# Attention and two expert layers on one core: the attention's last outputs and routing a tile sooner, fewer warm transposes, and split products in another order

## The chip, the cores and the metric

The kernel runs on one core of a Trainium2 chip. The metric is the device time of one execution in microseconds, as the median of several runs. The engines are named as in the profile: PE (TensorE), DVE (VectorE), ACT (ScalarE), POOL (GpSimd) and SP (the queue that issues most DMAs).

## The reference

Three layers stand behind one another. The attention is clustered: 2 batches, 8 heads, 768 tokens of 64 features, and a query sees only the keys whose nearest of 16 centroids is its own. Then every token goes to one of 8 experts (capacity 384), and a gated layer follows.

```python
q_assign = np.argmax(np.einsum('bhsd,hcd->bhsc', q_n, c_n), axis=-1)
k_assign = np.argmax(np.einsum('bhsd,hcd->bhsc', k_n, c_n), axis=-1)
mask = q_assign[:, :, :, None] == k_assign[:, :, None, :]
scores = np.where(mask, scale * np.matmul(q, k.transpose(0, 1, 3, 2)), -1000000000.0)
attn = softmax(scores)
x = np.matmul(attn, v)                       # (1536 tokens, 512)
logits = x @ w_gate                          # 8 experts
expert_idx = np.argmax(logits, axis=1)
...
h = np.maximum(np.einsum('ecd,edf->ecf', disp, w1), 0.0)
y = np.einsum('ecf,efd->ecd', h, w2)         # out[i] = gate_w[i] * y[...]
...
g = x @ w_gate; val = x @ w_val              # gated layer, 1536 wide
out = (g * sigmoid(g) * val) @ w_out
```

## The kernel before, in words

The order of the work is written out by hand; each engine runs its instructions in the order in which the program issues them.

**Start** (`Attention.run`, from line 430). After 16 warm transposes on PE (`warm`, line 424, transposes of the identity whose result nobody reads), `tr0` (line 166) transposes q and then k of the first pair of heads and makes three copies of each: X, in full precision, for the cluster assignment; H, the rounded high part; and L = X - H, on POOL. `moves` copies H and L into the operands Aq, qB, Ak and kB by DMA on SP's queue. `assign0` multiplies X with the centroids and makes a one-hot on DVE, `tr0` does the second pair's q, 28 more warm transposes follow, and `mask0` (line 259) transposes the one-hot (tile otp) and writes it into qB and kB as extra rows that mask the scores. Then the loop starts.

**The loop** (from line 491) goes over 96 tiles g of 128 queries; a group of three tiles is half a head, and eight pairs of heads make 96. In each tile the tokens of `CFG["order"]` are worked off: S is the exponential P of tile g+1 on ACT; E evacuates a finished product (ACT's `ol`, DVE's O); Q is the scores s of tile g+2 on PE and their maximum nm on DVE; T0 and T1 transpose P on PE (tile t, a pool `ps_t` of two buffers) and copy it out to PT, by ACT (T0) and by DVE (T1); O is the output `onat` (line 404); V0 is the product of P and V in the first tile of each group. `CFG["oc"]` says how many tiles behind its group the output comes, its third entry for the first half of the last pair.

**Output and routing.** `onat` multiplies O with an identity and the gate on PE (tile on) and scales it on DVE into two tensors: lg, the logits of that pair, and x. When the last pair of a batch is done for one half, `after` creates a routing chain (`Router.route`, line 614) for a quarter of the tokens: some twenty small DVE steps (rlo, rmx, rt, ... rslot, cnt, sum), an exponential on ACT, four small matmuls on PE into a tile of `ps_t`, and then for three times 128 tokens a scaling of x on ACT (line 666) and an indirect DMA on POOL that scatters the rows to `moe_rows`. Such a chain is a generator; `trickle` runs one step of it after each token listed in `CFG["mt"]`, or in `CFG["mt2"]` in the last pair's tiles (from 84 on), from the tile on that `CFG["ms"]` gives; the scalings and scatters run after token V0. What is left when the loop ends is run behind the last product.

**The experts** (`Experts.run`) load the scattered rows, transpose them (X, split into a high part by ACT and a low part by DVE) and multiply with W1 and W2, which are split as well: each product is high by high, high by low and low by high (`prod`, line 841). At the end comes the gated layer (`Glu`), which the change does not touch.

Of the kernel before, what the change touches and what calls it, by code (L numbers as in the profile page):

```python
# [14 lines left out]
AF = mybir.ActivationFunctionType  # L15
# [8 lines left out]
class Attention:  # L24
# [118 lines left out]
    def tr(self, n, nm, half):  # L143
# [10 lines left out]
        nc.scalar.activation(out=Ht[:, sl], in_=flat, func=AF.Copy, scale=s)  # L154
        if CFG["xe"]["qk".index(nm)] == "a":
            nc.scalar.activation(out=X[:, sl], in_=flat, func=AF.Copy, scale=s)
# [9 lines left out]
    def tr0(self, n, nm):  # L166

        nc, st = self.nc, self.pairs[n]
        J, HS = self.J, self.S // 2
        self.parts(n, nm)  # L170
        ps = self.ps_s.tile([128, 2, 512], F32, tag="s", name="s")
        for j in range(J):
            c = j % (J // 2) * 128
            nc.tensor.transpose(ps[:, 2 * j // J, c:c + 128], st[nm][:, j].rearrange("p r d -> p (r d)"), self.ident)
        Ht, Lt, X, s = (st[t + nm] for t in "HLXs")
        halves = lambda t: t.rearrange("p (a f) -> p a f", a=2)
        nc.scalar.activation(out=halves(X), in_=ps[:, :, 0:HS], func=AF.Copy, scale=s)
        nc.scalar.activation(out=halves(Ht), in_=ps[:, :, 0:HS], func=AF.Copy, scale=s)
        nc.gpsimd.tensor_tensor(out=Lt, in0=X, in1=Ht.bitcast(F32), op=ALU.subtract)

    def moves(self, n, r, names="qk"):

# [218 lines left out]
        if half == 1:  # L401
            del self.heads[hd]

    def onat(self, n, half):
        nc = self.nc
        J, D, E = self.J, self.D, self.E
        HJ = J // 2
        b, hp = divmod(n, self.H // 2)
        st = self.pairs[n]
        js = slice(half * HJ, (half + 1) * HJ)  # L410
        rs = self.p2.tile([128, HJ, 2], F32, name="rs")
        yield nc.vector.tensor_scalar(out=rs, in0=st["sum"][:, js], scalar1=1e-9, scalar2=None, op0=ALU.add)
        yield nc.vector.reciprocal(out=rs, in_=rs)
        ps = self.ps_m.tile([128, HJ, 2 * (D + E)], F32, tag="mm", name="on")
        for jj in range(HJ):
            j = half * HJ + jj
            nc.tensor.matmul(ps[:, jj, :], lhsT=st["O"][:, j * 128:(j + 1) * 128], rhs=self.R[:, hp, :],
                             start=True, stop=True)
        for dst, c, w in ((self.lg[:, b, js, 2 * hp:2 * hp + 2, :], 2 * D, E),
                          (self.x[:, b, js, 2 * hp * D:2 * (hp + 1) * D].rearrange("p j (r d) -> p j r d", r=2), 0, D)):  # L420
            yield nc.vector.tensor_tensor(out=dst, in0=ps[:, :, c:c + 2 * w].rearrange("p j (r d) -> p j r d", r=2),
                                          in1=rs.unsqueeze(3).to_broadcast([128, HJ, 2, w]), op=ALU.mult)

# [6 lines left out]
    def run(self, cent, gate, early, fill, after):  # L430
        nc = self.nc
        J = self.J
        HJ = J // 2
# [3 lines left out]
        for n in range(1, self.NP):  # L437
            s0 = 2 * J * (n - 1)
            st = self.prep_steps(n)
            for nm, o in CFG["offs" if n > 1 else "offs1"]:  # L440
                if n == 1 and nm in ("q0", "q1"):
                    continue
                bg.setdefault(s0 + o, []).append(st[nm])
            if n + 1 < self.NP:
                bg.setdefault(s0 + CFG["load"], []).append(lambda n=n: self.load(n + 1, "qk"))
            if n > 1:
# [1 line left out]
        self.warm(self.ps_m, "mm", 16)  # L448
        self.fixed()
        self.centroids()  # L450
        for nm in "qk":
            self.tr0(0, nm)
            if nm == "q":
                self.blocks()
        self.moves(0, 0)
        self.load(0, "v")
        self.moves(0, 1)
# [1 line left out]
        a = [self.assign0(0), self.assign0(1)]  # L459
        for i in (0, 0, 1, 0, 1, 0, 1, 0, 1, 1):  # L460
            next(a[i])
        self.tr0(1, "q")
        self.warm(self.ps_m, "mm", 28)
        self.mask0(0)
        self.mask0(1)
        self.moves(1, 0, "q")
# [11 lines left out]
        for G in range(4 * self.NP - 1):  # L478
            n, half, r = self.group(G)
            if r == 1:  # L480
                outs[(G + 1) * HJ + CFG["oc"][half if n + 1 < self.NP else 2]] = n, half

# [8 lines left out]
        for g in range(NG):  # L491
            G, c = divmod(g - HJ, HJ)
            steps = bg.pop(g, [])
            for tok in CFG["order"]:
# [8 lines left out]
                elif tok == "O" and g in outs:  # L503
                    n, half = outs[g]
                    for _ in self.onat(n, half):
                        pass
                    r = after(n, half)
# [12 lines left out]
        G, n = 2 * NH - 1, self.NP - 1  # L520
# [4 lines left out]
            moves.append(r)  # L525
        self.warm(self.ps_s, "s", 14)
        self.evac(G)
        for _ in self.onat(n, 1):
            pass
        for r in moves:  # L530
            for _ in r:
# [2 lines left out]
            pass  # L534


CFG = {'px': 'a', 'mt2': ['T0', 'S'], 'mt': ['B1'], 'pt': 'V0', 'pe': 1, 'ms': [5, 2, 1], 'mr': 5, 'order': ['S', 'E', 'Q', 'T0', 'T1', 'B0', 'O', 'V0', 'B1'], 'offs': [['k0', -3], ['q0', -2], ['q1', -1], ['k1', 0], ['a', 1], ['t', 3], ['f', 6], ['m0', 7], ['m1', 8]], 'xe': 'da', 'me': 'a', 'ee': 'a', 'ec': 1, 'oc': [5, 5, 2], 'offs1': [['q0', 4], ['k0', 0], ['k1', 1], ['a', 2], ['t', 3], ['f', 5], ['m0', 6], ['m1', 7], ['q1', 0]], 'load': 0}


class Router:  # L540
# [220 lines left out]
class Experts:  # L761
# [77 lines left out]
                                    op=ALU.subtract)  # L839

    def prod(self, out, W, ks, cols, mov):
        n, i = len(ks) * 3, 0
        for k in ks:
            for a, b in ((0, 0), (0, 1), (1, 0)):
                self.nc.tensor.matmul(out, lhsT=W[a][:, k, cols], rhs=mov[b][:, k, :], start=i == 0, stop=i == n - 1)  # L845
                i += 1

    def l1(self, mp, Hh, tag):
        nc = self.nc
# [353 lines left out]
```

## Time and profile before

| what | us |
|---|---|
| runs | 804.24, 801.65, 802.30; median 802.3 |
| the profiled execution | 802.64 |
| its span, first to last instruction | 800.9 |
| PE busy | 778.7 |
| DVE busy | 527.1 |
| ACT busy | 388.1 |
| POOL busy | 191.8 |

The profiled execution is one run of its own, and its rows add up to its span. A row of the timeline gives the start in us from the span's start, the time taken, the engine, the line, the operation, what it writes and reads, and in brackets how long the engine was idle before and what ended that.

### The profile page before, as it was taken

The numbers are of one execution on the slowest core, as the hardware profiler recorded it, in microseconds if no ns is written. First come the engines' busy times: TensorE is split into PE (matmuls) and PEld (weight loads), VectorE is DVE, ScalarE is ACT, GpSimd is POOL, SyncE is SP. The second block draws the span as 40 slices with busy tenths as digits, with TensorE's granted clock in tenths as the row PEclk, the third lists the DMA queues.
The fourth block names the chain that finished last, engine by engine and source line by source line (L and its number), as shares of the span: only waits on it lengthen the run. The fifth ranks groups of instructions, "written<-read, shape, count | busy, mean of one in ns | idle before, by whom it ended". The sixth has DMA issues, their size and how long they took to land. (4 is left out here: it accounts for less than half of the span.)

```text
span 800.9 us, 12676 instructions
## 1 busy us (share of the span) xinstructions
PE 778.7 (97%) x4791; PEld 654.7 (82%) x4791; DVE 527.1 (66%) x871; ACT 388.1 (48%) x704; POOL 191.8 (24%) x212
## 2 busy tenths in 40 slices
PE   8999999999999989999999999999999999999996
PEld 8677777767767679999999988778888888888885
DVE  3767867878777657565656644787766776676433
ACT  4776777777776535455545443354222232222210
POOL 5121211210211365000000001344333233323234
PEclk8999999999999999999999999999999999999999
DMA  9847867735640276666765641233121122210012
GB/s 204 198 94 206 206 182 202 165 72 134 146 154 28 80 259 215 195 192 213 229 208 189 191 127 54 82 100 109 54 80 52 56 77 67 66 54 1 0 53 105
DMA packets 93313, 102.03 MB, mean 127 GB/s; under 512 B 30304, under 2 KB 77408, under 8 KB 93248
## 3 DMA queue, kind: packets, MB, share of 16 engines
q1 hardware_dynamic: 88384, 89.33, 39.8%
q0 software_dynamic: 1920, 6.29, 2.1%
q10 hardware_dynamic: 2944, 5.54, 2.0%
q8 instruction: 41, 0.67, 0.4%
q14 instruction: 24, 0.20, 0.1%
HBM read 68.21 MB, written 12.58 MB: 101 GB/s over the span
## 5 line engine op out<-in xcount | busy, mean ns | idle before, releaser
L342 DVE TENSOR_REDUCE nm<-s 128x1 f32<-128x768 f32 x96 | 91.1, 950 | 11.5 <-PE s L339 10.6
L352 ACT ACTIVATE P<-s,nm 128x768 f32<-128x768 f32 x96 | 86.6, 902 | 13.4 <-DVE nm L342 10.4
L368 PE MATMUL t<-ident,P 128*128 128x128 f32 x576 | 81.2, 274 | 0.9 <-ACT PT L371 0.6
L1028 POOL TENSOR_TENSOR W1l<-cm,W1h 128x512 fp32r<-128x512 f32 x18 | 23.4, 1300 | 235.0 <-ACT W1h L1027 235.0
L368 PEld LDWEIGHTS t<-ident,P 128*128 128x128 f32 x576 | 68.5, 141 | 7.7 <-DVE PT L373 2.5
L845 PE MATMUL yp<-Hhh,W2h 128*128 128x256 f32 x256 | 73.1, 285 | 0.0
L845 PE MATMUL hp<-Xl,W1h 128*128 128x256 f32 x256 | 72.5, 283 | 0.3 <-DVE Xl L838 0.3
L845 PE MATMUL hp<-Xh,W1h 128*128 128x256 f32 x256 | 72.6, 284 | 0.2 <-ACT Xh L837 0.2
L845 PE MATMUL yp<-Hhh,W2l 128*128 128x256 f32 x256 | 72.5, 283 | 0.0
L845 PE MATMUL yp<-Hhl,W2h 128*128 128x256 f32 x256 | 72.4, 283 | 0.0
L845 PE MATMUL hp<-Xh,W1l 128*128 128x256 f32 x256 | 72.4, 283 | 0.0
L387 PE MATMUL acc<-PT,ldv 128*64 128x384 f32 x384 | 69.7, 495 | 0.0
L1055 POOL TENSOR_TENSOR ghl<-u,ghh 128x512 fp32r<-128x512 f32 x36 | 49.9, 1387 | 75.6 <-ACT ghh L1054 75.6
L339 PE MATMUL s<-Ak,Aq 128*128 128x384 f32 x192 | 58.5, 385 | 3.4 <-ACT P L352 3.1
L1074 DVE TENSOR_TENSOR acc<-o,acc 128x512 f32<-128x512 f32 x60 | 41.2, 692 | 30.4 <-PE o L1066 30.4
L1052 DVE TENSOR_TENSOR u<-sg,g 128x512 f32<-128x512 f32 x36 | 24.8, 688 | 54.8 <-ACT sg L1051 53.5
L371 ACT COPY PT<-t 128x384 f32<-128x384 f32 x96 | 45.8, 477 | 29.3 <-PE t L368 29.2
L1054 ACT CAST ghh<-u 128x512 fp32r<-128x512 f32 x36 | 22.4, 622 | 68.1 <-DVE u L1053 68.1
L373 DVE COPY PT<-t 128x384 f32<-128x384 f32 x96 | 52.4, 546 | 0.9 <-PE t L368 0.9
L339 PEld LDWEIGHTS s<-Ak,Aq 128*128 128x128 f32 x192 | 29.0, 189 | 28.2 <-ACT P L352 20.2
L339 PE MATMUL s<-kB,qB 80*128 80x384 f32 (+1 forms) x192 | 50.1, 341 | 1.0 <-ACT kB L274 0.7
L812 DVE TENSOR_TENSOR W2l<-raw,W2h 128x1024 fp32r<-128x1024 f32 x32 | 39.2, 1226 | 16.4 <-ACT W2h L811 15.8
(269 smaller groups left out, 1986.8 us busy)
## 6 DMA issues: line engine op xcount, KB each, us to landing
raw<-in_moe_w SPq DMA_DIRECT2D x64, 512.0 KB, 4.4
Ak<-Hk SPq DMA_DIRECT2D x32, 192.0 KB, 4.4
moe_rows<-zero SPq DMA_DIRECT2D x8, 768.0 KB, 5.5
raw<-in_moe_w_gate SPq DMA_DIRECT2D x12, 512.0 KB, 3.5
raw<-in_moe_w_val SPq DMA_DIRECT2D x12, 512.0 KB, 3.6
raw<-in_moe_w_out SPq DMA_DIRECT2D x12, 512.0 KB, 3.4
xr<-moe_rows ACTq DMA_DIRECT2D x7, 768.0 KB, 6.3
ldq<-in_q SPq DMA_DIRECT2D x16, 192.0 KB, 4.5
```

Source lines behind the costliest of these rows:

```text
L339: nc.tensor.matmul(ps[:, c, 0:HS], lhsT=ql[:, qs], rhs=kr[:, c * HS:(c + 1) * HS], start=a == 0, stop=a == 1)
L342: nc.vector.tensor_reduce(out=nm, in_=ps[:, :, 0:HS], axis=AX.XY, op=ALU.max, negate=True)
L352: nc.scalar.activation(out=P, in_=ps[:, :, 0:HS], func=AF.Exp, bias=nm, accum_out=self.pairs[n]["sum"][:, i, r:r + 1])
L368: nc.tensor.transpose(ps[:, jj, :], P[:, a, jj * 128:(jj + 1) * 128], self.ident)
L371: nc.scalar.copy(out=PT[:, js, cs], in_=ps)
L373: nc.vector.tensor_copy(PT[:, js, cs], ps)
L387: nc.tensor.matmul(acc[c * D:(c + 1) * D], lhsT=v[:, c * HJ + j], rhs=PT[:, c * HJ + j, :], start=j == 0, stop=j == HJ - 1, tile_position= ...
L812: nc.vector.tensor_tensor(out=l, in0=t, in1=h.bitcast(F32), op=ALU.subtract)
L845: self.nc.tensor.matmul(out, lhsT=W[a][:, k, cols], rhs=mov[b][:, k, :], start=i == 0, stop=i == n - 1)
L1052: nc.vector.tensor_tensor(out=u, in0=sg, in1=ps[0], op=ALU.mult)
L1055: nc.gpsimd.tensor_tensor(out=hl[:, fc], in0=u, in1=hh[:, fc].bitcast(F32), op=ALU.subtract)
L1074: nc.vector.tensor_tensor(out=a, in0=p[t], in1=a, op=ALU.add)
```

## The change

It has four parts.

1. `tr0` becomes a generator with a stop behind X. At the start X of q and X of k are made first, then H and L of q, then H and L of k.
2. The second group of warm transposes has 8 instead of 28.
3. In the last pair the first half's output comes at tile 91 instead of 92 (`oc` 2 to 1), its routing starts in the tile of the output instead of one behind (`ms` 1 to 0), and the steps run after four tokens of a tile, S, T0, T1 and V0, instead of after T0 and S. The second quarter's chain, which is under way at tile 84, goes by the same four tokens. The very last output's x is scaled by ACT in six pieces of 128x64 (`last=True`) instead of by one operation of DVE.
4. `prod` orders a product's matmuls by `high_first`: for each k high by high and low weight by high input, and behind all of these the products with the input's low part.

```diff
--- before.py
+++ after.py
@@ -175,8 +175,10 @@
         Ht, Lt, X, s = (st[t + nm] for t in "HLXs")
         halves = lambda t: t.rearrange("p (a f) -> p a f", a=2)
         nc.scalar.activation(out=halves(X), in_=ps[:, :, 0:HS], func=AF.Copy, scale=s)
+        yield
         nc.scalar.activation(out=halves(Ht), in_=ps[:, :, 0:HS], func=AF.Copy, scale=s)
         nc.gpsimd.tensor_tensor(out=Lt, in0=X, in1=Ht.bitcast(F32), op=ALU.subtract)
+        yield
 
     def moves(self, n, r, names="qk"):
 
@@ -401,7 +403,7 @@
         if half == 1:
             del self.heads[hd]
 
-    def onat(self, n, half):
+    def onat(self, n, half, last=False):
         nc = self.nc
         J, D, E = self.J, self.D, self.E
         HJ = J // 2
@@ -418,6 +420,12 @@
                              start=True, stop=True)
         for dst, c, w in ((self.lg[:, b, js, 2 * hp:2 * hp + 2, :], 2 * D, E),
                           (self.x[:, b, js, 2 * hp * D:2 * (hp + 1) * D].rearrange("p j (r d) -> p j r d", r=2), 0, D)):
+            if last and c == 0:
+                for jj in range(HJ):
+                    for r in range(2):
+                        nc.scalar.activation(out=dst[:, jj, r], in_=ps[:, jj, r * D:(r + 1) * D], func=AF.Copy,
+                                             scale=rs[:, jj, r:r + 1])
+                continue
             yield nc.vector.tensor_tensor(out=dst, in0=ps[:, :, c:c + 2 * w].rearrange("p j (r d) -> p j r d", r=2),
                                           in1=rs.unsqueeze(3).to_broadcast([128, HJ, 2, w]), op=ALU.mult)
 
@@ -448,10 +456,12 @@
         self.warm(self.ps_m, "mm", 16)
         self.fixed()
         self.centroids()
-        for nm in "qk":
-            self.tr0(0, nm)
-            if nm == "q":
-                self.blocks()
+        t = [self.tr0(0, nm) for nm in "qk"]
+        next(t[0])
+        self.blocks()
+        next(t[1])
+        for i in t:
+            next(i)
         self.moves(0, 0)
         self.load(0, "v")
         self.moves(0, 1)
@@ -459,8 +469,9 @@
         a = [self.assign0(0), self.assign0(1)]
         for i in (0, 0, 1, 0, 1, 0, 1, 0, 1, 1):
             next(a[i])
-        self.tr0(1, "q")
-        self.warm(self.ps_m, "mm", 28)
+        for _ in self.tr0(1, "q"):
+            pass
+        self.warm(self.ps_m, "mm", 8)
         self.mask0(0)
         self.mask0(1)
         self.moves(1, 0, "q")
@@ -525,7 +536,7 @@
             moves.append(r)
         self.warm(self.ps_s, "s", 14)
         self.evac(G)
-        for _ in self.onat(n, 1):
+        for _ in self.onat(n, 1, True):
             pass
         for r in moves:
             for _ in r:
@@ -534,7 +545,7 @@
             pass
 
 
-CFG = {'px': 'a', 'mt2': ['T0', 'S'], 'mt': ['B1'], 'pt': 'V0', 'pe': 1, 'ms': [5, 2, 1], 'mr': 5, 'order': ['S', 'E', 'Q', 'T0', 'T1', 'B0', 'O', 'V0', 'B1'], 'offs': [['k0', -3], ['q0', -2], ['q1', -1], ['k1', 0], ['a', 1], ['t', 3], ['f', 6], ['m0', 7], ['m1', 8]], 'xe': 'da', 'me': 'a', 'ee': 'a', 'ec': 1, 'oc': [5, 5, 2], 'offs1': [['q0', 4], ['k0', 0], ['k1', 1], ['a', 2], ['t', 3], ['f', 5], ['m0', 6], ['m1', 7], ['q1', 0]], 'load': 0}
+CFG = {'px': 'a', 'mt2': ['S', 'T0', 'T1', 'V0'], 'mt': ['B1'], 'pt': 'V0', 'pe': 1, 'ms': [5, 2, 0], 'mr': 5, 'order': ['S', 'E', 'Q', 'T0', 'T1', 'B0', 'O', 'V0', 'B1'], 'offs': [['k0', -3], ['q0', -2], ['q1', -1], ['k1', 0], ['a', 1], ['t', 3], ['f', 6], ['m0', 7], ['m1', 8]], 'xe': 'da', 'me': 'a', 'ee': 'a', 'ec': 1, 'oc': [5, 5, 1], 'offs1': [['q0', 4], ['k0', 0], ['k1', 1], ['a', 2], ['t', 3], ['f', 5], ['m0', 6], ['m1', 7], ['q1', 0]], 'load': 0}
 
 
 class Router:
@@ -839,11 +850,9 @@
                                     op=ALU.subtract)
 
     def prod(self, out, W, ks, cols, mov):
-        n, i = len(ks) * 3, 0
-        for k in ks:
-            for a, b in ((0, 0), (0, 1), (1, 0)):
-                self.nc.tensor.matmul(out, lhsT=W[a][:, k, cols], rhs=mov[b][:, k, :], start=i == 0, stop=i == n - 1)
-                i += 1
+        steps = self.high_first(ks)
+        for i, (k, b, a) in enumerate(steps):
+            self.nc.tensor.matmul(out, lhsT=W[a][:, k, cols], rhs=mov[b][:, k, :], start=i == 0, stop=i == len(steps) - 1)
 
     def l1(self, mp, Hh, tag):
         nc = self.nc
```

`high_first` was there before, for another product:

```python
def high_first(self, ks):
    return [(k, a, b) for a, bs in ((0, (0, 1)), (1, (0,))) for k in ks for b in bs]
```

**ACT at the start**, before and then changed (s is the PSUM tile of the transposes, Xq and Xk the full copies, Hq and Hk the high parts, kB the mask rows):

```order
L80 ACTIVATE re<-nrm 128x1
L177 ACTIVATE Xq<-s 128x768
L178 ACTIVATE Hq<-s 128x768
L177 ACTIVATE Xk<-s 128x768
L178 ACTIVATE Hk<-s 128x768
L177 ACTIVATE Xq<-s 128x768
L178 ACTIVATE Hq<-s 128x768
L274 ACTIVATE kB_89<-otp,sc 16x384 x2
```

```order
L80 ACTIVATE re<-nrm 128x1
L177 ACTIVATE Xq<-s 128x768
L177 ACTIVATE Xk<-s 128x768
L179 ACTIVATE Hq<-s 128x768
L179 ACTIVATE Hk<-s 128x768
L177 ACTIVATE Xq<-s 128x768
L179 ACTIVATE Hq<-s 128x768
L276 ACTIVATE kB_89<-otp,sc 16x384 x2
```

The full copy of k has moved ahead of the high part of q.

**DVE in tiles 91 to 93 of the loop**, before and then changed (nm is the maximum of two tiles on, PT the copy of this tile, the four rows from rs to x the output of the first half of the last pair, rlo, rmx, rt and rm the first steps of the third quarter's routing):

```order
L373 COPY PT<-t 128x3x128
L342 TENSOR_REDUCE nm<-s 128x1
L373 COPY PT<-t 128x3x128
L412 TENSOR_SCALAR rs<-sum 128x6
L413 RECIPROCAL rs<-rs 128x6
L421 TENSOR_TENSOR lg<-on,rs 128x3x16
L421 TENSOR_TENSOR x<-on,rs 128x3x128
L631 TENSOR_REDUCE rlo<-lg 128x24
L342 TENSOR_REDUCE nm<-s 128x1
L632 TENSOR_REDUCE rmx<-rlo 128x3
L373 COPY PT<-t 128x3x128
```

```order
L375 COPY PT<-t 128x3x128
L414 TENSOR_SCALAR rs<-sum 128x6
L415 RECIPROCAL rs<-rs 128x6
L429 TENSOR_TENSOR lg<-on,rs 128x3x16
L429 TENSOR_TENSOR x<-on,rs 128x3x128
L642 TENSOR_REDUCE rlo<-lg 128x24
L643 TENSOR_REDUCE rmx<-rlo 128x3
L344 TENSOR_REDUCE nm<-s 128x1
L644 TENSOR_TENSOR rt<-rlo,rmx 128x24
L375 COPY PT<-t 128x3x128
```

The output and two steps of the routing have moved ahead of one maximum nm and one copy PT.

**ACT behind the loop's last tile**, before and then changed (ol is the evacuation of the last product, x<-on the last output, x<-x,rgw the scaling of a quarter's tokens, the third quarter's and then the last quarter's, rd the last quarter's exponential):

```order
L371 COPY PT<-t 128x3x128 x2
L638 ACTIVATE rd<-rd 128x24
L398 COPY ol<-acc 64x384
L666 ACTIVATE x<-x,rgw 128x512 x3
L638 ACTIVATE rd<-rd 128x24
L666 ACTIVATE x<-x,rgw 128x512 x3
L811 CAST W1h<-raw 128x4x256 x4
```

```order
L373 COPY PT<-t 128x3x128 x2
L400 COPY ol<-acc 64x384
L426 ACTIVATE x<-on,rs 128x64 x6
L677 ACTIVATE x<-x,rgw 128x512 x3
L649 ACTIVATE rd<-rd 128x24
L677 ACTIVATE x<-x,rgw 128x512 x3
L822 CAST W1h<-raw 128x4x256 x4
```

Six scalings of the last output now stand between ol and the third quarter's scalings; the third quarter's own exponential has moved up into the loop.

## Rows read from the trace of the kernel before

**Rows 1.** The page, part 1: busy us of each engine (share of the span), instructions.

```profile
PE 778.7 (97%) x4791; PEld 654.7 (82%) x4791; DVE 527.1 (66%) x871; ACT 388.1 (48%) x704; POOL 191.8 (24%) x212
```

**Rows 2.** PE's waits between 24 and 262 us: total us, times, longest.

```profile
PE s L339 <- ACT P L352: 1.8, 6, 0.4
```

**Rows 3.** Timeline of the start: us from the span's start, us taken.

```profile
6.93 0.85 PE L174 MATMUL s<-ident,ldk 128*128 128x128 f32 x6 [0.48 <-DMA ldk<-in_k]
...
7.09 0.81 ACT L178 ACTIVATE Hq<-s 128x768 fp32r<-128x768 f32 x1
...
7.82 0.81 ACT L177 ACTIVATE Xk<-s 128x768 f32<-128x768 f32 x1
...
9.74 1.82 POOL L179 TENSOR_TENSOR Lk<-Xk,Hk 128x768 fp32r<-128x768 f32 x1
...
11.59 0.86 SPq L131 DMA_DIRECT2D kB<-Lk  x1
...
12.14 5.30 PE L428 MATMUL warm<-ident 128*128 128x128 f32 x28
...
13.14 0.36 DVE L255 TENSOR_TENSOR oh<-eq,m 128x192 f32<-128x192 f32 x1
...
17.28 0.82 PE L269 MATMUL otp<-ident,oh 128*64 128x128 f32 x6
...
19.11 1.00 PE L339 MATMUL s<-kB,qB 80*128 80x384 f32 x2 [0.66 <-ACT kB L274]
...
22.18 0.62 PE L339 MATMUL s<-Ak,Aq 128*128 128x384 f32 x2 [1.36 <-ACT P L352]
```

**Rows 4.** Stretches of half a microsecond; PEclk, the granted clock, stands before DMA share.

```profile
9.50:10.00 0.50, 0.50 (x5) 0.50 (x4) 0.33 (x1) 0.00 (x0) 0.50 (x2) 0.56 0.93 198
...
16.00:16.50 0.50, 0.50 (x4) 0.50 (x3) 0.00 (x0) 0.00 (x0) 0.50 (x2) 0.61 0.92 338
```

**Rows 5.** Tile kB before 24 us: its DMAs, from issue to landing.

```profile
DMA to landing us min/median/max: 2.8/3.9/4.7
```

**Rows 6.** Timeline, DVE in the attention's tiles 91 to 93.

```profile
257.52 0.55 DVE L373 COPY PT<-t 128x384 f32<-128x384 f32 x1
...
257.98 0.95 DVE L342 TENSOR_REDUCE nm<-s 128x1 f32<-128x768 f32 x1
...
258.84 0.55 DVE L373 COPY PT<-t 128x384 f32<-128x384 f32 x1
...
259.31 0.16 DVE L412 TENSOR_SCALAR rs<-sum 128x6 f32<-128x6 f32 x1
...
260.80 0.95 DVE L342 TENSOR_REDUCE nm<-s 128x1 f32<-128x768 f32 x1
```

**Rows 7.** Timeline of the attention's end and the last routing.

```profile
268.05 0.48 ACT L398 COPY ol<-acc 64x384 f32<-64x384 f32 x1 [1.95 <-PE acc L387]
...
268.43 1.95 ACT L666 ACTIVATE x<-x,rgw 128x512 f32<-128x512 f32 x3
...
269.86 0.55 DVE L400 TENSOR_TENSOR O<-acc,ol 64x384 f32<-64x384 f32 x1
...
271.51 0.21 DVE L421 TENSOR_TENSOR lg<-on,rs 128x48 f32<-128x48 f32 x1 [0.67 <-PE on L417]
...
271.63 0.55 DVE L421 TENSOR_TENSOR x<-on,rs 128x384 f32<-128x384 f32 x1
...
273.81 0.22 ACT L638 ACTIVATE rd<-rd 128x24 f32<-128x24 f32 x1 [3.43 <-DVE rd L637]
...
276.43 0.95 POOL L602 DMA_INDIRECT moe_rows<-x,rslot  x1 [2.58 <-ACT x L666]
...
278.95 2.00 POOL L602 DMA_INDIRECT moe_rows<-x,rslot  x1 [0.21 <-ACT W1h L811]
```

**Rows 8.** The chain of waits in order of time: start, us, what.

```profile
448.39 11.52 PE yp L845 x96
```

**Rows 9.** Timeline, the experts' first two products on PE.

```profile
287.98 0.39 PE L845 MATMUL hp<-Xh,W1h 128*128 128x256 f32 x1 [0.24 <-ACT Xh L837]
...
288.70 0.39 PE L845 MATMUL hp<-Xl,W1h 128*128 128x256 f32 x1 [0.34 <-DVE Xl L838]
```

## The prediction

> **What bounds the kernel now.** I read the page first. PE is busy for 97% of the span [rows 1], so a part of the change pays only where PE waits, or where PE does work that nobody needs. The list of PE's waits says where that is not: between 24 and 262 us, nearly all of the attention, PE's largest wait, for ACT's exponentials, comes to 1.8 us in six pieces [rows 2]. So that loop runs at PE's pace, and whatever starts it sooner ends it sooner by the same amount. Then I read the timeline at both ends of the attention. Before the loop the reader is to see 28 idle transposes of PE ending where the first transposes of the masks begin, and the low parts and their copies far from late [rows 3]. After the loop one chain runs: the last head's output, the routing of the last quarter of the tokens, its three scatters on POOL, the load of those rows, the first expert product. There the reader is to see what stands ahead of each step in its engine's queue [rows 7], and the gap between the first two products [rows 9].
>
> **The start.** The 28 warm transposes take 5.30 us, 0.19 each; 8 take 1.5 us and end at 13.7 where the mask's transposes now start at 17.28; their input, DVE's one-hot, is written by then [rows 3]. That would be 3.6 us. What is late next? The new order on ACT puts the k copy in full precision ahead of the high part of q. The k copy gains nothing: PE's transposes of k end at 7.78 and the copy starts at 7.82 already [rows 3]. But the high part of q moves from 7.09 to 8.53, by 1.4 us, and POOL's two low parts and SP's six copies behind it move too: the last low part, now 9.74 to 11.56, becomes 11.2 to 13.0, and the last copy of the first head (kB from Lk) is issued at 13.0 instead of 11.59 [rows 3]. At the median of 3.9 us from issue to landing [rows 5] it lands at 16.9. By the mask alone, the second half of the first scores could start at 13.7 + (19.11 - 17.28) = 15.5. So the copy decides, and those scores start at 16.9 instead of 19.11: 2.2 us sooner (3.3 and 1.4 at the extremes of rows 5). SP's later copies for the second head slip by the same 1.4 us; they are first read at tile 6, some 9 us into the loop, and I cost them nothing: if that cover went, PE would wait for them there, at most 1.4 us.
>
> The 28 transposes have a second effect. The granted clock falls at 9.5 us to half (1.2 of 2.4 GHz) and comes back at 16.4, near the end of this dense stretch of transposes [rows 4]. With 8 of them PE is dense only to about 15, then waits for a copy. The Trainium skill's page "TensorE: Matmul & The Clock Gate", section "What's actually happening", says that the slow clock is the default and that activity releases it; by that rule cutting warm work delays the release, and the trace agrees as far as one return during 28 transposes goes. What it costs, from rows: the loop's dense part starts at 22.18 - 2.2, about 20.0; if the low clock lasts another stretch as long as the one of rows 4 (6.8 us, to 23.2), 3.2 us of dense work run at half speed, which loses 1.6. So the start is worth between -2.2 and -0.6. Neither end has the nearer row, and I take -1.4.
>
> **The last pair's output one tile sooner.** DVE's order at tiles 91 to 93 now has the first half's output (rs, its reciprocal, lg, x) and the first steps of the third quarter's routing between tile 92's PT copy and the maximum nm of tile 95: 259.31 to 260.80, 1.5 us [rows 6]. That maximum is not urgent; PE has a whole product of P and V to do first. In the change they stand ahead of the maximum of tile 94 and so ahead of tile 92's PT copy, which goes from 258.84 to about 260.4. PE's next transposes need that buffer of two; they wait some 0.8 us more. Later the third quarter's position matmuls take one of the same two buffers between tiles 94 and 95, and the last transposes wait for DVE's product of them: about another 0.7, by one PT copy of 0.55 and a small step of 0.16 [rows 6]. So the last product of P and V comes later by up to 1.5. Against it, the routing's tail no longer stands in front of DVE's last O: O started at 269.86 although ACT's ol was ready at 268.53 [rows 7], so 1.3 us come back. The four steps a tile instead of two also finish the second quarter sooner; PE is not held by that, by rows 2, and I cost it at nothing. Together: +0.2, and -1.3 if DVE's slack hides the delay.
>
> **The last output on ScalarE.** DVE's x (0.55, between lg and the routing) goes away: the routing starts about 0.4 sooner [rows 7]. Its six replacements read the same PSUM tile behind DVE's lg, which ends at 271.72. Each takes between 0.22, the routing's 128x24 exponential, and 0.48, the 64x384 copy ol [rows 7]; 128x64 is nearer the first, and I take 0.25: 1.5 us, to 273.2. Queued behind them on ACT are the third quarter's three scalings, which ran at 268.43 (1.95 for three, 0.65 each), under PE's last product and O; they now run from 273.2 to 275.2. Two things wait for them. The exponential of the last routing goes from 273.81 to 275.2, +1.4, and DVE's later steps follow it. POOL's scatters: the third quarter's first can start near 274.0, behind the first scaling; at 1.26 a scatter (276.43 to 278.95 for two [rows 7]) the last quarter's first follows three later, at 277.8 instead of 276.43, +1.4. The two run side by side, so the chain pays 1.4. With +0.2 and -0.4 the last scatter is 1.2 us later. The bounds: -1.7, if both delays are hidden (-1.3 - 0.4); -0.3, if DVE's alone is; +2.6, if each of the six takes 0.48. I take +1.2.
>
> **High parts first.** The first expert product starts at 287.98; the second, with X's low part, waits for DVE until 288.70. The pace of these products is 0.12 (96 in 11.52 us [rows 8]), so 0.6 is lost [rows 9]. In the new order eight products of the high part stand first, and the low part is ready when they end. So -0.6. For the other products the inputs are ready long before; the number of matmuls and weight loads does not change (every matmul has its own load, as many loads as matmuls [rows 1]), and I cost the order itself at nothing.
>
> **Sum.** -1.4 + 1.2 - 0.6 = -0.8. The profiled execution took 802.64 us (its span of 800.9 and 1.7 around it), 0.3 above the median of 802.3; so 801.8 by the profiled one, 801.5 by the median. I say 801.7. No change within 0.3% (2.4 us, about what a measurement of this kernel can tell) is 799.9 to 804.7.
>
> **The rivals.**
> - *The tail is a gain.* DVE has slack at tile 92, the transposes do not wait, and POOL's six scatters fit: -1.7, with the full -2.2 at the start and -0.6: -4.5, 797.8. For it: the loop hides nearly all waits of PE [rows 2]. Against it: the third quarter's scalings stand behind the six new activations on ACT whatever DVE does.
> - *The clock stays low.* This is the side of slower. Each microsecond of the loop at 1.2 GHz beyond 20.0 costs half a microsecond of PE. If the fewer transposes leave it low until 30 us, the start is -2.2 + 5.0 = +2.8, and with +1.2 and -0.6 the time is 3.4 above the median, 805.7. It decides from about 28 us on: -2.2 + 4.0 + 0.6 = +2.4. Against it: PE is dense from 20 us, and it came back once in 6.8 us.
> - *The scatters themselves get slower.* The last scatter took 2.00 us, against 0.95 for the first of its quarter [rows 7], while DVE was already splitting W1. With all three of the last quarter later, the first two can meet that split as well: 2.1 us more, 803.6. The Trainium skill's "SBUF — State Buffer", section "SBUF: two separate sides", has such a rule: VectorE with two SBUF inputs and GpSimd lock each other out of a shared port. The trace agrees at most in part: the first and the last of the three start 2.52 us apart, so the one between was not slowed [rows 7].
> - *The change does not do what it says.* The k copy "sooner" is not sooner; this is already in the sum.
>
> **How the numbers follow.** The forecast, a start and a tail that nearly cancel: 0.58; its own range is -2.2 to -0.6 for the start, -0.3 to +2.6 for the tail and -0.6, so 799.2 to 803.7. The gain in the tail 0.22, the low clock 0.10, slower scatters 0.10. Faster by over 0.3% is the gain in the tail and the lowest edge of the forecast: 0.24. Slower by over 0.3% is the clock with a little of the scatters: 0.12. The rest, 0.64, is no measurable change. The range that holds 8 in 10 reaches half way to the gain and over the slow scatters: 798.6 to 804.8.
>
> **What would show it.** Right: the first scores with kB start near 17 us, waiting for a DMA and not for ACT; the granted clock comes back later than 16.5; PT of tile 92 about 1.5 us later against its scores, with a wait of PE on DVE of about a microsecond; O directly behind ol; ACT's three scalings behind six short x; POOL's six scatters without a gap; and no gap between the first two expert products. Wrong: a loop that starts at 15.5, a clock back by 16.4 in spite of all, or scatters of the third quarter that start before the last output.

## The result: slower, and the profile after

The changed kernel took 807.7 us (median of 6 runs, 805.9 to 808.4), the kernel before beside it 802.0 (801.6 to 804.2). The ratio is 1.0062, with a 95% interval of 1.0045 to 1.0078: slower by some 5 us, where no measurable change was forecast. The profiled execution has a span of 806.6 us against 800.9, so 5.7 us have to be found.

I followed the same markers through both traces, and read where the changed kernel falls behind:

| marker | before, us | after, us | difference | gained or lost since the marker above |
|---|---|---|---|---|
| masks' first transposes (otp) | 17.28 | 15.89 | -1.39 | -1.39 |
| exponential of tile 0 | 21.14 | 19.99 | -1.15 | +0.24 |
| exponential of tile 4 | 28.86 | 30.01 | +1.15 | +2.30 |
| exponential of tile 87 | 241.97 | 244.75 | +2.78 | +1.63 |
| last scatter starts | 278.95 | 283.63 | +4.68 | +1.90 |
| first expert product | 287.98 | 292.80 | +4.82 | +0.14 |
| end of the span | 800.9 | 806.6 | +5.7 | +0.88 |

So there are four losses: at the start (1.2 instead of a gain of 1.4), inside the loop (1.6), at the tail (1.9), and at the experts' first products (0.9). After those products nothing more is lost: the chunk of [rows 8] starts at 454.12, 5.73 later, as the span.

The page, part 1, of the changed kernel, beside [rows 1]: PE has 20 matmuls fewer and is busy 0.9 us less, so it is waits or slow work that cost.

```profile
PE 777.8 (96%) x4771; PEld 654.6 (81%) x4771; DVE 530.6 (66%) x870; ACT 389.2 (48%) x710; POOL 192.7 (24%) x212
```

**The start.** The timeline of the changed kernel, beside [rows 3]: start, us taken.

```profile
10.80 1.04 PE L436 MATMUL warm<-ident 128*128 128x128 f32 x8
11.05 1.93 POOL L180 TENSOR_TENSOR Lk<-Xk,Hk 128x768 fp32r<-128x768 f32 x1
...
11.76 1.43 DVE L255 TENSOR_TENSOR eq<-eq,desc 128x192 f32<-128x192 f32 x1
...
12.94 1.91 POOL L180 TENSOR_TENSOR Lq<-Xq,Hq 128x768 fp32r<-128x768 f32 x1
...
13.12 1.95 DVE L257 TENSOR_TENSOR oh<-eq,m 128x192 f32<-128x192 f32 x1
...
15.89 0.81 PE L271 MATMUL otp<-ident,oh 128*64 128x128 f32 x6 [4.05 <-DVE oh L257]
...
17.71 1.24 PE L341 MATMUL s<-kB,qB 80*128 80x384 f32 x2 [0.39 <-ACT kB L276]
```

The transposes end at 11.84, and then PE waits 4.05 us for DVE's one-hot. The prediction had it "written by then". Two DVE steps that take 0.35 each in the profile before take 1.43 and 1.95. Each began while POOL computed a low part, and each ended about 0.2 after that low part did (11.05 + 1.93 = 12.98 against 13.19; 12.94 + 1.91 = 14.85 against 15.07). The Trainium skill's page "SBUF — State Buffer", section "SBUF: two separate sides", says that a VectorE operation with two SBUF inputs and a GpSimd operation that reads SBUF shut each other out for the whole instruction. These rows agree, on both sides: POOL's two low parts, each begun while such a DVE step ran, took 1.93 and 1.91, and 1.81 where none ran. The prediction weighed that rule at the scatters only.

Then the clock, in windows of the changed kernel. The column after POOL's is the granted clock.

```profile
14.00:17.00 3.00, 1.11 (x8) 0.96 (x8) 2.29 (x5) 0.00 (x0) 2.80 (x8) 0.93 0.97 234
17.00:20.00 3.00, 2.61 (x8) 1.75 (x6) 2.48 (x4) 2.45 (x5) 0.56 (x7) 0.50 0.93 248
20.00:24.00 4.00, 3.21 (x13) 2.88 (x13) 1.92 (x3) 2.45 (x5) 0.00 (x0) 0.50 0.93 218
24.00:28.00 4.00, 4.00 (x21) 3.87 (x20) 2.07 (x3) 2.80 (x7) 1.00 (x1) 0.64 0.67 161
```

In the profile before the half clock lay at 9.6 to 16.4, mostly over idle transposes [rows 4]. Here it falls at about 16.6, behind the 4 us of waiting, and returns at 26.8 (0.64 over the last 4 us is 2.9 of them at half). It covers the loop's first tiles, and between tiles 0 and 4 the lead of 1.15 becomes a lag of 1.15. Other profiles of the same start have the half clock elsewhere (`hf`, below), so the first rows of the table hold for these two executions.

**Inside the loop.** PE's waits between 24 and 262 us, beside [rows 2], have a new entry: 1.7 us in two waits for the small copies from oT, at 142 and 236, at boundaries between pairs of heads.

```profile
PE s L341 <- DMA kB<-oT: 1.7, 2, 0.9
```

**The tail**, beside [rows 7], in order of time.

```profile
272.21 0.55 DVE L402 TENSOR_TENSOR O<-acc,ol 64x384 f32<-64x384 f32 x1 [1.98 <-ACT ol L400]
...
274.12 0.21 DVE L429 TENSOR_TENSOR lg<-on,rs 128x48 f32<-128x48 f32 x1 [0.93 <-PE on L419]
274.36 1.34 ACT L426 ACTIVATE x<-on,rs 128x64 f32<-128x64 f32 x6 [2.18 <-DVE lg L429]
...
275.55 1.97 ACT L677 ACTIVATE x<-x,rgw 128x512 f32<-128x512 f32 x3
...
276.58 0.96 POOL L613 DMA_INDIRECT moe_rows<-x,rslot  x1 [20.63 <-DVE ret L652]
...
277.39 0.24 ACT L649 ACTIVATE rd<-rd 128x24 f32<-128x24 f32 x1
...
280.37 0.96 POOL L613 DMA_INDIRECT moe_rows<-x,rslot  x1 [0.23 <-ACT x L677]
281.27 4.63 DVE L823 TENSOR_TENSOR W1l<-raw,W1h 128x1024 fp32r<-128x1024 f32 x4 [1.83 <-ACT W1h L822]
...
281.64 1.69 POOL L613 DMA_INDIRECT moe_rows<-x,rslot  x1 [0.22 <-issue]
...
283.63 1.97 POOL L613 DMA_INDIRECT moe_rows<-x,rslot  x1 [0.21 <-issue]
```

As forecast, O stands directly behind ol, the scalings behind six short x, the exponential behind the scalings, and six scatters follow each other. What the sum left out: with the quarter's scatters later, two of them, not one, run beside DVE's split of W1, and take 1.69 and 1.97 instead of 0.96.

**The experts.** First products of the changed kernel, beside [rows 9]:

```profile
292.80 0.39 PE L855 MATMUL hp<-Xh,W1h 128*128 128x256 f32 x1 [0.24 <-ACT Xh L848]
293.03 0.35 PE L855 MATMUL hp<-Xh,W1l 128*128 128x256 f32 x1
293.18 0.42 PE L855 MATMUL hp<-Xh,W1h 128*128 128x256 f32 x1
293.39 0.42 PE L855 MATMUL hp<-Xh,W1l 128*128 128x256 f32 x1
```

The gap of 0.7 between the first two is gone, but from 293.1 on they follow each other at 0.21 instead of 0.12, until 296.5: the granted clock is at half again (0.50 in this window), behind a wait of PE for the rows of 3.0 us.

```profile
294.00:295.00 1.00, 1.00 (x7) 1.00 (x6) 0.07 (x1) 0.45 (x1) 1.00 (x1) 0.50 0.99 344
```

### The profile page after: what moved, and what is told of

It reads as the page before. It is cut to its first block, busy times and chain, and to the rows that moved or that the text cites. A ratio compares the mean times of both kernels' runs of the same rounds, so it can differ in the third digit from the quotient of the medians.

```text
span 806.6 us, 12641 instructions
## 1 busy us (share of the span) xinstructions
PE 777.8 (96%) x4771; PEld 654.6 (81%) x4771; DVE 530.6 (66%) x870; ACT 389.2 (48%) x710; POOL 192.7 (24%) x212
## 5 line engine op out<-in xcount | busy, mean ns | idle before, releaser
L855 PE MATMUL hp<-Xh,W1h 128*128 128x256 f32 x256 | 65.4, 287 | 0.2 <-ACT Xh L848 0.2
L855 PE MATMUL hp<-Xh,W1l 128*128 128x256 f32 x256 | 65.2, 286 | 0.0
L855 PE MATMUL yp<-Hhh,W2h 128*128 128x256 f32 x256 | 63.5, 286 | 0.0
L855 PE MATMUL yp<-Hhh,W2l 128*128 128x256 f32 x256 | 62.8, 283 | 0.0
L855 PEld LDWEIGHTS hp<-Xh,W1h 128*128 128x128 f32 x256 | 50.0, 195 | 0.5 <-ACT Xh L848 0.5
L855 PEld LDWEIGHTS hp<-Xh,W1l 128*128 128x128 f32 x256 | 50.1, 196 | 0.0
L855 PEld LDWEIGHTS yp<-Hhh,W2l 128*128 128x128 f32 x256 | 49.2, 192 | 0.0
```

## The experiments

Theory A: the start (transposes, one-hot, clock), the copies at the boundaries, and the ACT queue at the tail cost what the table shows. The rivals stand with each run. "Later" and "sooner" are against the kernel before in its profile, as in the table. The kernel before, run beside these kernels, had medians of 802.45 (`w8`, `w28`, `oldtail`, `hf`), 802.64 (`w20`, `hold`, `dveo`, `ofirst`), 802.82 (`best`, `hffill`) and 802.28 (`best2`, `afterfill`).

### The start: transposes, order of the copies, clock

`w8`, the kernel before with fewer transposes:

```
-        self.warm(self.ps_m, "mm", 28)
+        self.warm(self.ps_m, "mm", 8)
```

> The kernel before, with 8 instead of 28 warm transposes ahead of the masks and nothing else. Theory A (the fewer transposes move the half-clock stretch from the idle start into the first tiles): the masks' transposes start some 3 us sooner, the granted clock is at 0.5 in the first tiles of the loop, and the loop is later by about 1 from tile 4 on, as in the changed kernel: 803.2. Rival B (the loss at the start comes from the new order of the k and q copies, which lets POOL's low parts run beside DVE's one-hot): here DVE's one-hot stays quick, the loop starts 1 to 2 us sooner and keeps it: 800.5.

Measured: 804.07, ratio 1.0022 (1.0008 to 1.0036). PE of its profile:

```profile
13.82 0.82 PE L269 MATMUL otp<-ident,oh 128*64 128x128 f32 x6 [0.43 <-DVE oh L255]
...
14.84 0.59 PE L339 MATMUL s<-Ak,Aq 128*128 128x384 f32 x2 [0.20 <-DMA Aq<-Lq]
```

The masks start at 13.82, 3.46 sooner and where the prediction's arithmetic put them (13.7); the one-hot takes 0.36 here. The half clock lay at 10.2 to 13.7, not in the first tiles, and at 801.8 this was the fastest of the 12 runs. The loop has 3.45 of the lead at tile 4 and 2.29 at tile 87; the 1.16 goes at the boundaries between pairs, at the oT copies, as in the changed kernel. Another 1.45 goes at the experts, where the clock falls as it does there. Over all 12 runs the granted clock was 0.990 to 0.995, mean 0.9925, against 0.989 to 0.999, mean 0.9948, of the 35 runs of the kernel before. Both theories are half right: the one-hot stays quick and the loop starts sooner, but in the median of the runs the kernel is 1.6 later. By the price of the half clock (0.37 us for each, from the runs of the kernel before; last section) the lower mean clock is worth 0.0023 x 2 x 802 x 0.37 = 1.4 of that, an estimate.

The 3.46 is luck in part, and so is the 3.6 that the prediction worked out: the 5.30 us of the 28 transposes [rows 3] were taken at half clock. `hf`, further down, starts as the kernel before does, and its clock is at full over these steps and on to 19.8:

```profile
10.75 3.22 PE L428 MATMUL warm<-ident 128*128 128x128 f32 x28
...
12.61 1.95 POOL L179 TENSOR_TENSOR Lq<-Xq,Hq 128x768 fp32r<-128x768 f32 x1 [0.99 <-ACT Hq L178]
...
13.19 1.59 DVE L255 TENSOR_TENSOR oh<-eq,m 128x192 f32<-128x192 f32 x1
...
14.93 0.82 PE L269 MATMUL otp<-ident,oh 128*64 128x128 f32 x6 [0.96 <-DVE oh L255]
```

The 28 transposes take 3.22, end at 13.97, and the masks wait for the one-hot. They start 2.35 sooner than in the profile before, with no edit to the start; against `hf`, `w8` gains 1.1. The one-hot is slow here too, with the copies in the old order: POOL's low part of the second pair's q starts at 12.61, against 14.04 in the profile before, and the one-hot meets it. So it does in `ofirst` (1.61), `best` (1.85) and `hffill` (1.99), all in the old order. It takes 0.36 only in the kernel before, `w8` and `best2`, whose half clock began at about 10 us. So the new order is not the only cause of the slow one-hot. Where the clock is full over these steps, the masks start at 14.73 to 15.16 in the old order (four profiles) and at 15.85 to 16.21 in the new (five): the new order costs about 1 us there. Where the half clock began at about 10, the one-hot is done at 13.67 in `w8` and at 15.58 in `w28`, 1.9 later.

`w28`, the changed kernel with 28 transposes (the same line, the other way round):

> The changed kernel with 28 warm transposes again. Theory A: the half-clock stretch lies in the transposes again, the one-hot of DVE (ready near 15.8) is hidden behind them, and the loop is at most 0.3 later than in the kernel before where it was 1.2 later: 1.0 to 1.5 less than the changed kernel, 806.4. Rival B: the slow one-hot still delays the masks, or the clock falls in the first tiles all the same: 807.7, as the changed kernel.

Measured: 805.49, ratio 1.0033 (1.0021 to 1.0044). A's time was too high and its step wrong: in the profile the half clock came twice, at 9.9 to 13.3 and again at 20.1 to 27.0, and the loop was still 1.0 later at tile 4. What rival B describes happened, though not at its time. And the loop was 1.0 later at tile 87 too: the waits for the oT copies were gone. Neither theory foresaw that, and the next run asks why.

### Inside the loop: a fetch of instructions

`w20`, the changed kernel with 20 transposes:

> The changed kernel with 20 warm transposes in place of 8. In three profiles with 8 of them (this change, the kernel before with 8, and the change with the old tail) an instruction fetch of 16 KB falls on the issue of the small oT copies at both boundaries between pairs of heads, an issue of 0.6 takes 1.0 to 1.5, and PE waits there 0.5 to 0.9 twice; with 28 the fetch comes some 4 us sooner and misses them. Theory A (the place of the fetch in the stream of PE's instructions decides): 12 more transposes move it 2.3 us ahead, it ends just before the issues, and both waits go: 1.5 less than the changed kernel, 806.2. Rival B (the slow issues are chance, or come from something else in the start): the waits stay, 807.7.

Measured: 805.33, ratio 1.0038 (1.0026 to 1.0051); 0.93 later at tile 87 as at tile 4. SP's issues at the first of the two late boundaries, the changed kernel:

```profile
137.86 2.15 SPq L131 DMA_DIRECT2D qB<-oT  x2
140.06 1.22 SPq L131 DMA_DIRECT2D kB<-oT  x2
```

and in the run with 20:

```profile
137.63 1.23 SPq L131 DMA_DIRECT2D qB<-oT  x2
138.90 1.22 SPq L131 DMA_DIRECT2D kB<-oT  x2
```

The DMA queues of the changed kernel between 137.86 and 141.28 hold, beside these copies, one packet of the instruction queue (count, MB, share); the same stretch of the kernel before and of this run holds none.

```profile
q8 instruction: 1, 0.02, 2.0%
```

Such a packet, 16 KB in about 1.1 us, comes every 13 to 24 us in the 14 profiles. In the changed kernel one starts at 138.55 and one at 232.27; with 20 transposes at 134.91 and 227.67, ahead of the issues. Of all issues of oT copies in the loop, in all 14 profiles, each that took over 0.7 us a copy (0.6 is usual) has such a packet beside it, and none is slow without one, while a few that are touched by a packet are not slow. Removing 20 matmuls from PE's stream moved the packets some 4 us against the loop (134.50 in `w28`, 138.55 in the changed kernel), onto two boundaries; the 12 of `w20` moved them by 3.6 where 2.3 was expected. That slow issues go with a packet, and that the waits went when the packets were moved, is shown; why a packet holds up SP's issue is not.

### The tail

`oldtail`, the changed kernel with the old tail:

```
-'mt2': ['S', 'T0', 'T1', 'V0'] ... 'ms': [5, 2, 0] ... 'oc': [5, 5, 1]
+'mt2': ['T0', 'S'] ... 'ms': [5, 2, 1] ... 'oc': [5, 5, 2]
-        for _ in self.onat(n, 1, True):
+        for _ in self.onat(n, 1):
```

> The changed kernel with the old schedule of the last pair (three entries of the table) and the last output on DVE again; start and products as changed. Theory A (the tail costs 2.5, and the longer wait for the first expert's rows lets the clock fall, 1.5 more): the last scatter stands where it did against the loop and the clock keeps its level at the first products: 4 us less than the changed kernel, 803.7. Rival B (the fall of the clock there is chance or a matter of the product order): only 2.5 less, 805.2.

Measured: 804.94, ratio 1.0028 (1.0018 to 1.0039). From tile 87 to the last scatter it loses nothing (1.92 and 1.93 later), so the whole 1.9 is the tail's. The clock does not fall at the first products, but the time that theory A gave for that did not come: rival B's is the nearer.

`dveo`, the changed kernel with the new schedule but the last output on DVE (only the last two lines of that diff):

> The changed kernel with the last output on DVE again (the six small activations go); the schedule of the last pair stays as changed. Theory A (on ACT the six put the third quarter's scalings, and with them the last routing's exponential and POOL's scatters, late): the scalings start right behind ol, the exponential comes 1.0 sooner, the third quarter's scatters run ahead of the last quarter's instead of into them, and the last scatter is 2.3 sooner against the loop: 805.4. Rival B (the last pair's schedule costs it, not ACT): the last scatter moves by at most 0.5, 807.4.

Measured: 804.71, ratio 1.0028 (1.0018 to 1.0038). Its tail:

```profile
272.26 1.95 ACT L677 ACTIVATE x<-x,rgw 128x512 f32<-128x512 f32 x3
...
273.26 0.96 POOL L613 DMA_INDIRECT moe_rows<-x,rslot  x1 [17.14 <-DVE rs L414]
...
276.59 0.22 ACT L649 ACTIVATE rd<-rd 128x24 f32<-128x24 f32 x1 [2.38 <-DVE roh L647]
...
279.20 0.96 POOL L613 DMA_INDIRECT moe_rows<-x,rslot  x1 [2.36 <-ACT x L677]
...
281.73 2.00 POOL L613 DMA_INDIRECT moe_rows<-x,rslot  x1 [0.21 <-ACT W1h L822]
```

The scalings run right behind ol, the third quarter's scatters are done before the last quarter's can start, and one scatter meets the split. From tile 87 (2.95 later) to the last scatter (2.78) the new schedule alone gains 0.2. Theory A's steps happened: the exponential comes 0.97 sooner against the loop, the last scatter 2.07. So the six activations on ACT cost 2.1, and the schedule nothing.

`ofirst`, a candidate for the old tail, with the high parts first:

```
+        self.evac(G)
         for _, r in chains:
...
         self.warm(self.ps_s, "s", 14)
-        self.evac(G)
```

> A candidate: the kernel before with the high parts first, and the last head's O put ahead of the rest of the third quarter's routing on DVE (by order of code alone; the table and the last output on DVE as before). Theory A (in the kernel before, O waits 1.3 for that routing although its input is ready): O starts 1.2 sooner against the loop, lg and the last scatter 0.6 sooner: 0.6 less than with the high parts alone, 800.8. Rival B (the third quarter's scatters, now later, push the last ones): no gain over the high parts alone, 801.4.

Measured: 802.25, ratio 0.9996 (0.9982 to 1.0010), no gain. O did start 1.3 sooner against the loop, but PE's position matmuls, which stand ahead of `on` in its queue, then waited for a step of DVE behind O (0.5 before):

```profile
PE t L651 <- DVE roh L636: 1.5, 1, 1.5
```

lg came 0.4 later against the loop. The rival that happened was a third one.

### The experts' products

`hf`, the kernel before with `prod` as in the change:

> The kernel before, with the high parts first in the products and nothing else. Theory A: the gap between the first two products goes, 0.6 less: 801.4. Rival B: the order costs or gains something in the other 32 products of 32 matmuls too; each 0.1 a product would be 3 us, so below 799 or above 803.

Measured: 801.40, ratio 0.9978 (0.9965 to 0.9991). Its first two products:

```profile
287.12 0.39 PE L844 MATMUL hp<-Xh,W1h 128*128 128x256 f32 x1 [0.24 <-ACT Xh L837]
287.34 0.28 PE L844 MATMUL hp<-Xh,W1l 128*128 128x256 f32 x1
```

From the first product to the end it gains 0.44 on the kernel before, the gap and nothing else; `w20`, `hold` and `dveo` gain 0.43 to 0.48 there as well (`oldtail` only 0.06, which no run explains). Theory A holds, with 0.44 where 0.6 was expected. The rest of the difference in medians goes with the clock: mean 0.996 in these 12 runs against 0.9948.

`hold`, the changed kernel with PE's wait for the rows filled:

```
-        for i in range(26):
+        for i in range(38):
```

> The changed kernel with 38 instead of 26 idle products of W1 ahead of the first expert's transposes; 12 more at 0.23 fill 2.8 of the 3.0 us in which PE waits there for the rows. Theory A (the clock falls at 293 because PE waited just before): the granted clock stays at 1.0 there in the profile, and what it cost, up to 1.5, comes back: 806.4. Rival B (the fall comes whatever PE does there): the half-clock stretch of 3.4 us is there again, 807.7, or 808.5 if the added products end after the rows land.

Measured: 806.85, ratio 1.0054 (1.0040 to 1.0068). The wait for the rows is 0.2, and the clock stays at 1.0 there. But it also stayed in `w20` with a wait of 2.8 and in `dveo` with 1.6, and it fell in `w8` with 1.7 and in `w28` with 2.8. So in the changed kernel's profile the fall cost about 1.3 (0.88 lost where 0.45 should be gained), and whether the longer wait makes it more frequent stays open: the runs don't tell.

### Filling the waits ahead of the loop

`best`, the kernel before with the high parts first and:

```
-        self.warm(self.ps_m, "mm", 28)
+        self.warm(self.ps_m, "mm", 20)
...
+        self.warm(self.ps_t, "t", 3)
         self.qk(0)
         self.soft(0)
         self.qk(1)
+        self.warm(self.ps_t, "t", 8)
```

> A candidate: the kernel before with the high parts first, 20 warm transposes, and 11 idle transposes in PE's two waits ahead of the loop (3 before the first scores, 8 before the loop); order of the copies, schedule and last output as before. Theory A (the half-clock stretch falls into the first tiles because PE waits just before; with the waits filled it stays out of them or is short): the runs' mean granted clock rises from 0.996 with the high parts alone to 0.997 or more, the loop starts 1 sooner for the fewer warm transposes, and the time is 799.9. Rival B (the stretch comes whatever PE does in those waits): clock as before, 801.0.

Measured: 800.27, ratio 0.9968 (0.9956 to 0.9981). The granted clock in its profile never falls between 5.4 and the last 2 us:

```profile
17.00:20.00 3.00, 2.39 (x16) 2.11 (x16) 2.42 (x4) 2.70 (x6) 0.10 (x3) 1.00 1.01 211
20.00:24.00 4.00, 3.85 (x29) 3.54 (x28) 2.85 (x4) 3.31 (x9) 1.00 (x1) 1.00 0.99 224
```

The mean over its 11 runs is 0.9983, against 0.9942 for the kernel before beside it. That is what theory A said: with PE's waits just ahead of the loop filled by eleven matmuls that compute nothing, the half clock stays out of the first tiles. Of the ten profiles without them it lay there in eight, also with 28 warm transposes in the old order (`hf`, `ofirst`); in none of the four with them.

`hffill`, the same with 28 transposes:

> The same with 28 warm transposes, so the high parts first and the 11 idle transposes alone against the run with the high parts alone. Theory A: a mean granted clock of 0.997 or more and 800.6. Rival B: 801.4 as with the high parts alone, at a clock of 0.996.

Measured: 801.72, ratio 0.9984 (0.9972 to 0.9996), at a mean clock of 0.9981. The clock is A's, the time B's, and the profile says why: now a fetch starts at 73.23, on the first boundary, and the loop loses 1.09 between tiles 4 and 87.

```profile
72.55 2.22 SPq L131 DMA_DIRECT2D qB<-oT  x2
```

`best2`, 16 and 3 + 6 transposes:

> The candidate with 16 warm and 9 idle transposes instead of 20 and 11. In the profile of the candidate an instruction fetch at 73.4 meets the copies at the first boundary between pairs and PE waits 0.6 there. Theory A: six instructions fewer push the fetch behind that boundary, the wait goes, and the fetch of the later boundaries still comes before them: 799.7. Rival B (16 transposes leave PE idle too long before the masks, and the clock falls in the first tiles in some runs): 800.8 at a mean clock below 0.997.

Measured: 800.11, ratio 0.9968 (0.9954 to 0.9982). No boundary is met, and the loop keeps its whole lead (3.03 sooner at tile 4, 3.02 at tile 87); but the mean clock is 0.9963, as rival B had it. The two effects cancel, and `best` and `best2` can't be told apart. Both beat the kernel before and the changed one.

`afterfill`, the changed kernel with 36 transposes and the same eleven:

> The changed kernel with 36 warm transposes and the 11 idle transposes ahead of the loop; order of the copies, schedule, last output and products as changed. It tests whether the parts add up. Theory A: the half-clock stretch leaves the first tiles, the fetch misses the two late boundaries, and what is left over the run with 28 and 11 (801.7) is the tail, 2.6, and the slower one-hot, 1.2, less 1.0 if no fetch meets a boundary: 804.4 at a mean clock of 0.996 or more. Rival B (something else in the change costs the time): 806 or more at that clock.

Measured: 804.59, ratio 1.0024 (1.0011 to 1.0038), mean clock 0.9961. The transposes and the filled waits together bring the changed kernel down by some 3 us. Of its profile's 2.9 over the kernel before, 1.9 is the tail (0.15 later at tile 87, 2.06 at the last scatter) and 0.95 the experts, where the clock falls. One boundary is still met by a fetch, at a cost of 0.9; with that the expected sum is 805.5, so the parts add up to within 1 us. The run changes the transposes and the fills at once and does not tell them apart.

## Why the prediction was wrong, step by step

- **"Their input, DVE's one-hot, is written by then."** This failed. The prediction itself moved POOL's low parts ("the last low part, now 9.74 to 11.56, becomes 11.2 to 13.0") and did not ask who runs beside them. The low part then ran from 11.05 to 12.98, with a second right behind it, and the masks waited for the one-hot until 15.89. The one-hot's time was also that of an execution at half clock: at full clock it takes 1.59 to 1.99 in the old order too, so the step would have failed there without the new order. The limit that the prediction put in its place, the kB copy at 16.9, did not decide: the scores at 17.71 waited for ACT's kB.
- **The 3.6 us of the transposes.** The sum is right for the row it was taken from, and `w8` has its masks 3.46 sooner than that profile. But at full clock 28 transposes take 3.22 and end before the one-hot (`hf`), so fewer of them gain nothing there.
- **The start is worth -1.4.** Measured: +1.15 at tile 4, with 2.3 lost to the clock between tiles 0 and 4. The clock was seen as a danger, at most 1.6 in the sum and a rival with a chance of 0.10 beyond; the granted clock came back at 26.8, not at 23.2. Of the 6.8 us at half clock from 20.0 on each cost 0.34, not the half that the prediction put. It had PE dense to about 15 and then waiting for a copy; PE waited 4 us for the one-hot from 11.84 on, and the clock fell at the end of that. Whether this wait brought the fall is not shown: no run fills it alone. Over many runs of the kernel before the price shows too: in the 35 runs beside `w8` it takes 800.2 to 800.3 at a mean clock of 0.998 to 0.999 and 803.2 to 804.6 at 0.993. The six runs of the changed kernel had a mean of 0.9903, 0.0045 below; at 0.37 for each microsecond at half clock that is 2.7 us of the loss, an estimate.
- **"whatever starts it sooner ends it sooner by the same amount."** This failed by 1.6: the oT copies at two boundaries came late, held up beside an instruction fetch, which no step looked at. The later copies for the second head, costed at nothing, did cost nothing: the list of PE's waits has no other new entry of their size.
- **The last pair's output, +0.2.** PE's wait for the PT copy is there, 1.2 us at 263.57 where 0.8 was said, and O starts directly behind ol, which gives 1.3 back. From tile 87 to the last scatter the schedule alone gained 0.2 (`dveo`), inside the bounds given.
- **The last output on ScalarE, -0.4 + 1.4.** The mechanism was right: routing 0.35 sooner, six x at 0.22 each where 0.25 was said, the exponential 1.3 later than the routing it belongs to. The size was off: 2.1 in place of 1.0, and 0.7 of that is the scatter of 1.69, not 0.96, beside DVE's split. The rival "the scatters themselves get slower" was this, with one scatter more and not two.
- **High parts first, -0.6.** Right: 0.44 in `hf`. In the changed kernel the half clock at the same place hid it.
- **The sum.** -0.8 was forecast and +5.7 measured in the profile: +1.2 at the start, +1.6 in the loop, +1.9 at the tail, +0.1 for the rows, and +0.9 at the experts.

## What to carry to other kernels

When a change moves an operation in time, look for what its new neighbours share with it, not only for who waits for it: here POOL's subtractions, once they fell beside DVE's two-input steps, stretched them from 0.35 to as much as 1.99. Before taking a price from a row, ask whether the row stands in every execution: the same start had its masks at 17.28 in one profile and at 14.73 to 15.16 in three others (`hf`, `ofirst`, `hffill`), depending on where the half clock lay. Idle matmuls ahead of a dense loop are not only a delay: eleven in PE's waits kept the half clock out of the loop's first tiles. And before moving small work to a free engine, read what stands behind it in that engine's queue: 1.3 us of ACT in front of three scalings became 2.1 at the end of a chain.

## What the runs showed that was not expected

- One kernel's time follows its granted clock. Each microsecond at half clock cost the kernel before about 0.37: between 0.999 and 0.993 lie 0.006 x 2 x 801 = 9.6 us of half clock and 3.6 us of time.
- A packet of the instruction queue, 16 KB in about 1.1 us, that falls on an issue of SP can lengthen it from 1.23 to 2.15 us for two copies. So twenty matmuls more or fewer at the start change waits 120 and 210 us later.
- DVE's product and one-hot took 0.72, 1.43 and 1.95 instead of 0.35 in the changed kernel, each time ending 0.2 behind POOL's low part; DVE's steps with one SBUF input, between them, kept their 0.34. In the old order it depends on the clock: 1.59 to 1.99 for the one-hot in four profiles, 0.36 in three.
- The clock fell at the experts' first products in 4 of the 14 profiles (the change, `w8`, `w28` and `afterfill`), behind waits of PE of 3.0, 1.7, 2.8 and 2.8 us, and did not in others with 1.7 and 2.8. What decides stays open.
